# W_out's block sums laid out by product, made over the first chunk of the second layer, and read into twelve buffers

## The chip, the cores and the metric

The kernel runs on one core of a Trainium2 chip. The metric is device time in microseconds (us) of one execution. The engines are TensorE (PE; its weight loads PEld run beside it), VectorE (DVE), ScalarE (ACT), GpSimd (POOL) and SyncE (SP, which here only issues DMAs); transfers run on 16 DMA engines.

## What is computed

Windowed attention over 4 batches x 8 heads x 576 positions x 64 elements, then two feed-forward layers on the 2304 x 512 result. All of it is float32.

```python
x = attention(q, k, v)                 # causal, window of 64; reshaped to [2304, 512]
h = x @ w_in                           # [512, 2048]
x = (h * sigmoid(h)) @ w_out           # [2048, 512]
h = x @ w_in2                          # second layer
g = where(h >= 1, h, where(h <= -1, 0, (h + 1)**2 / 4))
out = g @ w_out2                       # [2304, 512]
```

## The kernel before

**Products.** Every float32 operand is split into a high part of type fp32r and the rest (`hi_lo`, L758 for the rest; the high part is a copy, L261 on ACT or L263 on DVE), and a product is three matmuls: high by low, low by high, high by high. The weights of both layers come as pairs of 32-bit words and are converted once (`weight`, L315 to L385); the second layer's go to DRAM (`ws2`).

**Layer 1** takes the tokens in five chunks (512, 256, 512, 512, 512), with the attention between them. `step` (L676) multiplies by W_in (L688), applies the activation on ACT twice, once to float32 and once to fp32r (L698, L700), subtracts on DVE (L702) and multiplies by W_out (L722).

**Layer 2** takes the tokens in three chunks n of 768, in two halves of 384 (TH). W_in's product is a block product in seven products (tokens: `tokens_quarters`, weights: `weights_quarters`, with sums L762). In chunk n=0 the 2048 hidden units are taken in eight pairs (`pair`, L856): seven products of six matmuls (L872), sums on DVE (L880), the activation (L899 DVE, L901 ACT, L903 DVE, cast on ACT, L905 DVE), then a plain product with W_out (L944) whose weights are W_out's high and low parts. The block sums of W_in are stored in `a_dram` (L832) and read again (L816) for n=1 and n=2, whose first product is made phase by phase (L1020, sums L1028) before the second.

**W_out for n=1 and n=2.** Their second product is a block product in seven products too: `products_out` (L1089) runs 7 x 8 = 56 units of six matmuls (L1143), and each unit reads its own piece of W_out's block sums, high and low, of 256 KB. `weights_out(i)` makes them for pair i: it loads the two pieces of W_out (`wst`, L970), splits them (these parts also serve n=0's L944), forms four sums in place, splits those, and stores all of it in `e_dram` (L976). A unit's load (L1104) takes 256 of a row's 512 columns, high and low, so a partition's 2 KB lie in DRAM as two runs of 1 KB. The loads go round a ring of 7 buffers (`TAGS`), those of the first product's weights.

**The order** is set by a list scheduler (class `Plan`). Each operation has a key, made of its step's due time and a term of the table K; a cost on each engine that could run it; `lat`, what the planner adds for a DMA to land; and `after`, before which it isn't put. The planner puts at each moment the ready operation with the lowest key on each engine and writes one fixed order for each engine. So a waiting instruction holds all that stands behind it on its engine. The time in the plan decides the order alone; on the chip, semaphores do. `lead2` (102.98) lets W_out's loads for pair i start that many planned us before pair i's due time, and so in layer 1.

**Output.** Each finished tile is turned by DVE (L1111) and stored by four DMAs of 48 KB (L1116), on SP except for the very last.

Of the kernel before, what the change touches and what calls it, by code (L numbers as in the profile page):

```python
# [10 lines left out]
F32 = mybir.dt.float32  # L11
# [34 lines left out]
class Plan:  # L46
# [128 lines left out]
K = dict(wload=-19.78, rebias=0.22, low=-18.2, shift=-27.36, add=-0.16, sign=10.81, hi=-2.67, lo=-23.79, qkv=-15.09,  # L175
         v=1.07, qT=-26.02, kT=0.97, sc=-21.48, max=-20.9, exp=-6.11, sum=-40.26, tr=-13.39, pv=1.78, x=-11.84,
         f_max=-1.34, f_exp=29.66, f_sum=2.76, f_tr=21.88, f_pv=3.83, f_x=6.87, f_v=7.59, f_t0=-4.04, f_t1=6.08,
         f_t2=44.33, f_t3=13.71, f_a0=-25.21, f_a1=16.54, f_a2=20.65, f_a3=22.2, f_l0=-24.76, f_l1=-19.36, f_l2=4.46,
         f_l3=20.84, f_v0=-20.48, f_v1=-20.39, f_v2=0.67, f_v3=1.42, split=-8.01, x2=-61.84, act=13.29, sub=-6.21,
         out=3.75, w2=-6.13, t0=29.25, drift0=0.58, drift1=0.86, pu0=0.33, pu1=0.61, pu2=0.34, pu3=0.52, c1=30.89,  # L180
         stay=36.55, spare=4.5, evac=26.68, base2=-5.58, store=9.98, bhl=-13.0, bsub=7.66, aload=22.2, fload=-50.69,
         ahl=44.73, asum=24.32, astore=-7.2, add2=-12.87, act2=-4.15, sub2=8.31, out2=32.34, wi0=163.69,
         ahead2=-59.06, lead2=102.98, w22=-35.28, ehl=-5.54, esum=6.04, estore=-37.75, hadd=-26.88, hact=1.31,
         s1=8.57, ring=-3.45, osum=-51.98, oload=-55.71, oev=12.85, ostore=3.95, bq=56.81)
# [19 lines left out]
def tile_window_attention_two_ffn(  # L204
# [110 lines left out]
    def weight(layer, f, part, key, early, after=0.0):  # L315
# [49 lines left out]
        op(key + K["wload"], dict(sp=1.45 if part else 1.71), load, w=[hi, lo], makes=[st], lat=1.9, after=after)  # L365
# [404 lines left out]
    def tokens_quarters(n):  # L770

        at = lambda nm: T2[0] + PAIR * order[nm] / 7 if not n else H0[n] + UNIT * order1[nm] + K["bq"]
        key = H0[n]
        for a in range(2):
            x = {}
            for h in range(2):
                for kk in (a, a + 2):
                    nm = f"b{kk // 2 + 1}{h + 1}"
                    b = x[nm] = Buf(xp, "xf", [128, 512])
                    t0 = n * WIDE + h * TH  # L780
                    need = [item for p0, p1, item in x2_parts[kk] if p0 < t0 + TH and p1 > t0]
# [18 lines left out]
            keep("t2", x["b22"])  # L800
            keep("b21", x["b21"])
            minus("t4", x["b21"], x["b21"], x["b22"])
            keep("t4", x["b21"])

    def weights_quarters(n, i):
# [7 lines left out]
        if n:  # L813
            for nm, _ in IN_BANKS:
                y = aq[n, i, nm]
                op(at(nm) + K["aload"], dict(sp=0.35), lambda e, nm=nm: e.dma_start(out=whole(nm), in_=a_dram[i, nm][:, :]),  # L816
                   r=[("a", i, nm)], w=[(y, 0), (y, 1)], makes=[y], lat=2)
            return
        w = []
        for f in (2 * i, 2 * i + 1):  # L820
            b = Buf(wp, "wf", [128, 512])
            w.append(b)
            op(key + K["fload"], dict(sp=0.75), lambda e, b=b, f=f: e.dma_start(out=b.t, in_=ws2[0][f][:, :]),
               r=[("ws2", 0, f)], w=[(b, 0), (b, 1)], makes=[b], lat=2)
# [137 lines left out]
    e_dram = {(i, x): dram.tile([128, 2, 512], F32, name=f"e_{i}_{x}") for i in range(NF // 2) for x in range(4)}  # L962

    def weights_out(i):
# [10 lines left out]
        def store(x, y, halves):  # L975
            op(t + K["estore"], dict(sp=0.35), lambda e: e.dma_start(out=e_dram[i, x][:, :, 0:256 * halves],  # L976
                                                                    in_=y.t[:, :, 0:256 * halves].bitcast(F32)),
               r=[(y, 0), (y, 1)], w=[("e", i, x)], lat=2)

        store(0, wt[1, 2 * i, 1], 1)  # L980
        store(1, wt[1, 2 * i + 1, 1], 2)

# [8 lines left out]
        for x in range(2):  # L991
            y = Buf(wp, "w0", [128, 2, 512], F32R)
            hi_lo(t + K["ehl"], lambda part, y=y: y.t[:, part, :], lambda x=x: w.t[:, x, :], 512, [(w, x, 0), (w, x, 1)], (y,), [y])
            store(2 + x, y, 2)
# [91 lines left out]
    IN_OUT = dict(P1=(0, 0, 0), P5=(1, 2, 0), P6=(0, 3, 1), P7=(1, 2, 1), P2=(2, 1, 0), P3=(0, 1, 1), P4=(3, 3, 0))  # L1086
    TAGS = ((ap, "qn"), (ap, "kn"), (ap, "qT"), (ap, "kT"), (ap, "pT"), (ap, "pT"), (ap, "v"))

    def products_out(n):  # L1089
# [9 lines left out]
        for j, (q, x, half) in enumerate(products):  # L1099
            for i in range(NF // 2):  # L1100
                s = (NF // 2) * j + i
                pool, tag = TAGS[s % 7] if not (last and j == 6 and i == 7) else (xp, "xf")
                y = ew[j, i] = Buf(pool, tag, [128, 2, 256], F32R)
                op(at_o(n, j, i) + K["oload"], dict(sp=0.35), lambda e, y=y, i=i, x=x, half=half: e.dma_start(  # L1104
                    out=y.t.bitcast(F32), in_=e_dram[i, x][:, :, half * 256:half * 256 + 256]),
                   r=[("e", i, x)], w=[(y, 0), (y, 1)], makes=[y], lat=2)

        def store(j, m, src, r, c):
# [185 lines left out]
```

## Time and profile before

| | |
|---|---|
| median of 3 runs | 903.74 us (903.32 to 905.78) |
| the profiled execution, its own time | 902.7 us |
| its span, first to last instruction | 900.9 us |
| mean granted TensorE clock | 0.987 |
| busy: PE, DVE, ACT, POOL | 95%, 71%, 58%, 12% of the span |

The page of the profile gives busy times of the engines and the costliest groups of instructions. The trace behind it can be asked for windows (busy time of each engine in a stretch, the granted clock, the DMA engines' busy share), timelines (instructions of an engine in order, with the idle time ahead of each and what ended it), waits (that idle time summed by what ended it) and DMAs. By the timeline, layer 1 ends at about 511 us, chunk n=0 takes 493 to 636, n=1 to 772 and n=2 the rest; the layers overlap at 486 to 513.

### The profile page before, as it was taken

The numbers are of one execution on the slowest core, as the hardware profiler recorded it, in microseconds if no ns is written. First come the engines' busy times: TensorE is split into PE (matmuls) and PEld (weight loads), VectorE is DVE, ScalarE is ACT, GpSimd is POOL, SyncE is SP. The second block draws the span as 40 slices with busy tenths as digits, with TensorE's granted clock in tenths as the row PEclk, the third lists the DMA queues.
The fourth block names the chain that finished last, engine by engine and source line by source line (L and its number), as shares of the span: only waits on it lengthen the run. The fifth ranks groups of instructions, "written<-read, shape, count | busy, mean of one in ns | idle before, by whom it ended". The sixth has DMA issues, their size and how long they took to land.

```text
span 900.9 us, 16116 instructions
## 1 busy us (share of the span) xinstructions
PE 858.6 (95%) x5470; PEld 758.0 (84%) x5470; DVE 638.1 (71%) x1519; ACT 526.7 (58%) x1148; POOL 107.4 (12%) x111
## 2 busy tenths in 40 slices
PE   7899999999999999999998899999999998899996
PEld 6788778998778887888886798888899998899996
DVE  5899996655564367535677699778877984678951
ACT  6989987866675378733435444444566631567430
POOL 3100100100000000000000233113022010113010
PEclk9999999999999999999999899999999999999998
DMA  9952535654566056503678766438788789887786
GB/s 259 326 172 70 156 71 121 154 132 105 148 168 151 24 163 191 139 14 100 210 274 312 272 251 229 164 129 297 242 246 254 238 267 237 246 252 246 234 235 139
DMA packets 231602, 172.00 MB, mean 191 GB/s; under 512 B 141152, under 2 KB 191840, under 8 KB 231520
## 3 DMA queue, kind: packets, MB, share of 16 engines
q1 hardware_dynamic: 230320, 170.83, 63.7%
q8 instruction: 43, 0.70, 0.3%
q14 instruction: 39, 0.32, 0.1%
q10 hardware_dynamic: 1200, 0.15, 0.1%
HBM read 123.73 MB, written 47.19 MB: 190 GB/s over the span
## 4 chain that ended last, share of the span: by engine, by line
PE 54%; DMA 14%; ACT 13%; DVE 10%; SPq 6%; issue 3%; POOL 0%; DVEq 0%; ACTq 0%; POOLq 0%
PE acc L722 11%; PE h L688 11%; PE acc L1020 6%; PE acc L1143 6%; PE h L872 5%; PE at L1020 3%; PE acc L944 3%; DMA wst<-ws 2%; DMA w<-in_moe_w_in_dram 2%; ACT s L421 2%; PE at L1143 2%; PE h L1143 2%; DVE w L758 2%; ACT L421 2%; ACT wl L338 1%
## 5 line engine op out<-in xcount | busy, mean ns | idle before, releaser
L722 PE MATMUL acc<-g,w 128*128 128x512 f32 (+1 forms) x996 | 222.5, 367 | 0.0
L688 PE MATMUL h<-xt,w 128*128 128x512 f32 (+1 forms) x996 | 215.6, 364 | 1.8 <-ACT g L700 1.8
L688 PEld LDWEIGHTS h<-xt,w 128*128 128x128 f32 x996 | 169.6, 189 | 32.4 <-ACT g L700 3.0
L722 PEld LDWEIGHTS acc<-g,w 128*128 128x128 f32 x996 | 169.1, 190 | 29.5 <-issue 2.1
L702 DVE TENSOR_TENSOR g<-gf,g 128x512 fp32r<-128x512 f32 (+1 forms) x83 | 52.6, 634 | 44.6 <-ACT g L700 44.2
L698 ACT ACTIVATE gf<-h 128x512 f32<-128x512 f32 (+1 forms) x83 | 44.8, 540 | 55.7 <-PE h L688 55.3
L261 ACT CAST w<-w 128x384 fp32r<-128x384 f32 x75 | 36.8, 511 | 26.9 <-PE acc L1143 18.3
L421 ACT ACTIVATE s<-s,st 128x128 f32<-128x128 f32 x128 | 49.9, 392 | 4.2 <-DVE st L400 3.9
L417 POOL TENSOR_TENSOR s<-s,st 128x512 f32<-128x512 f32 (+1 forms) x16 | 15.8, 986 | 287.7 <-DVE st L414 163.0
L346 DVE CUSTOM_DVE_ANT_0 wf<-wf,wl 128x1024 uint16<-128x1024 uint16 x64 | 45.0, 704 | 2.3 <-ACT wl L338 1.4
L700 ACT ACTIVATE g<-h 128x512 fp32r<-128x512 f32 (+1 forms) x83 | 44.7, 538 | 2.8 <-PE acc L722 2.7
L1020 PE MATMUL acc<-w,pT 128*128 128x384 f32 x192 | 39.3, 340 | 2.5 <-DMA pT<-a_s 1.9
L758 DVE TENSOR_TENSOR w<-w,w 128x384 fp32r<-128x384 f32 x67 | 34.6, 548 | 7.7 <-ACT w L261 7.7
L338 ACT ACTIVATE wl<-wst 128x512 int32<-128x512 uint32 x32 | 21.5, 671 | 29.7 <-DMA wst<-in_moe_w_out_dram 12.8
L698 ACT ACT_TABLE_LOAD x27 | 34.6, 1283 | 5.1 <-PE h L688 4.6
L1020 PEld LDWEIGHTS acc<-w,pT 128*128 128x128 f32 x192 | 33.9, 188 | 3.8 <-DVE xt L1120 1.3
L421 ACT ACT_TABLE_LOAD x28 | 35.9, 1283 | 0.5
L880 DVE TENSOR_TENSOR xt<-h,xt 128x384 f32<-128x384 f32 x56 | 30.6, 552 | 6.5 <-PE h L872 5.7
L1028 DVE TENSOR_TENSOR w<-acc,xt 128x384 f32<-128x384 f32 x48 | 26.7, 556 | 11.2 <-PE acc L1020 10.0
L400 DVE CUSTOM_DVE_ANT_0 s<-at,mask 128x128 f32<-128x128 f32 x128 | 29.2, 282 | 6.2 <-PE at L531 6.2
L342 DVE TENSOR_SCALAR wf<-wf 128x512 int32<-128x512 int32 x48 | 20.2, 429 | 18.6 <-ACT wf L333 18.2
L944 PE MATMUL acc<-w,g 128*128 128x512 f32 x120 | 31.9, 393 | 0.1
(238 smaller groups left out, 1716.8 us busy)
## 6 DMA issues: line engine op xcount, KB each, us to landing
e<-w SPq DMA_DIRECT2D x24, 512.0 KB, 4.2
w<-in_moe_w_in_dram SPq DMA_DIRECT2D x16, 512.0 KB, 7.3
w<-in_moe_w_out_dram SPq DMA_DIRECT2D x16, 512.0 KB, 7.1
wst<-in_moe_w_in_dram SPq DMA_DIRECT2D x16, 512.0 KB, 4.3
ws<-wf SPq DMA_DIRECT2D x32, 256.0 KB, 4.4
wst<-in_moe_w_out_dram SPq DMA_DIRECT2D x16, 512.0 KB, 4.1
pT<-a_s SPq DMA_DIRECT2D x32, 256.0 KB, 3.1
pT<-e SPq DMA_DIRECT2D x32, 256.0 KB, 3.5
```

The lines of the kernel that those rows point to most:

```text
L346: e.tensor_tensor(out=i, in0=i, in1=wl.t, op=ALU.add)
L421: e.activation(out=s.t[:, jj, :], in_=s.t[:, jj, :], func=AF.Exp, scale=-1.0, bias=st.t[:, jj:jj + 1], accum_out=st.t[:, 4 + jj:5 + jj])
L688: e.matmul(out=h.t[:, 0:n], lhsT=w[:, a, kk, :], rhs=xt[layer, c, kk // 2].t[:, kk % 2, b, lo:hi], start=(kk == 0 and j == 0), stop=(kk == ...
L698: op(key, dict(act=t_act(n, True)), lambda e: e.activation(out=gf.t[:, 0:n], in_=h.t[:, 0:n], func=AF.Silu), r=[h], w=[gf], makes=[gf], ta ...
L700: op(key, dict(act=t_act(n, True)), lambda e: e.activation(out=g.t[:, 0, 0:n], in_=h.t[:, 0:n], func=AF.Silu), r=[h], w=[(g, 0)], makes=[g ...
L702: op(T[i] + K["sub"], dict(dve2=t_dve(n)), lambda e: e.tensor_tensor(out=g.t[:, 1, 0:n], in0=gf.t[:, 0:n], in1=g.t[:, 0, 0:n].bitcast(F32) ...
L722: e.matmul(out=acc[t].t[:, lo:hi], lhsT=wo.t[:, a, t * 128:(t + 1) * 128], rhs=g.t[:, b, 0:n], start=fresh and j == 0, stop=(j == 2 and f ...
L758: op(key, dict(dve2=t_dve(n), pool=0.18 + 2.17e-3 * n), lambda e: e.tensor_tensor(out=y(1), in0=src(), in1=y(0).bitcast(F32), op=ALU.subtr ...
L872: e.matmul(out=acc(nm), lhsT=y.t[:, p, a * 128:a * 128 + 128], rhs=bq[n, bn, a].t[:, q, :], start=(a == 0 and j == 0), stop=(a == 1 and j ...
L944: e.matmul(out=acc2[quarter % 2 * 3 + m].t, lhsT=y(p)[:, m * 128:m * 128 + 128], rhs=wo.t[:, q, :], start=(f == 0 and j == 0), stop=(f == ...
L1020: e.matmul(out=acc(nm), lhsT=y.t[:, p, a * 128:a * 128 + 128], rhs=bq[n, bn, a].t[:, q, :], start=(new and a == 0 and j == 0), stop=(a == ...
L1143: e.matmul(out=banks[j][m].t[:, 0:TH], lhsT=w.t[:, p, m * 128:m * 128 + 128], rhs=y.t[:, r, :], start=(j < 4 and i == 0 and k == 0), stop= ...
```

## The change

In words:

- `e_dram` is cut by product: each unit's piece, high and low, is one run of 2 KB for each partition. The three plain blocks B11, B21, B22 have tiles of their own, the sums lie with the half outermost (and are split into that order). Stores go from 32 to 40 of the same bytes in all.
- W_out's loads for pair i start `lead3` = 21.25 planned us before its due time instead of 102.98, so the block sums are made pair by pair over chunk n=0.
- The ring has 12 buffers: two of `wf`, one of `wl` and two of `gf` are added, which are free by then.
- The planner's costs: a DMA issue on SP 0.4 where 0.75 stood, `lat` 3 to 4 where 2 stood. Tokens of n=1 and n=2 are split no earlier than 22 us ahead of their chunk.
- K's numbers are others; among them `wi0` 163.69 to 211.15 (the second layer's weights are converted later in layer 1).
- Every output store may go on ACT's queue or SP's.

```diff
 # weight, second layer
-        op(key + K["wload"], dict(sp=1.45 if part else 1.71), load, ..., lat=1.9, after=after)
+        op(key + K["wload"], dict(sp=0.45 if layer else 1.45 if part else 1.71), load, ..., lat=3.8 if layer else 1.9, after=after)
 # tokens_quarters
-                hi_lo(at(nm) + K["bhl"], ..., TH, [src], (y,), [y])
+                hi_lo(at(nm) + K["bhl"], ..., TH, [src], (y,), [y],
+                      H0[n] - 22 if n else 0.0)
 # weights_quarters
-            op(key + K["fload"], dict(sp=0.75), ..., lat=2)
+            op(key + K["fload"], dict(sp=0.4), ..., lat=3.4)
 # weights_out
-    e_dram = {(i, x): dram.tile([128, 2, 512], F32, ...) for i in range(NF // 2) for x in range(4)}
+    e_dram = {(i, x): dram.tile([128, 2, 2, 256], F32, ...) for i in range(NF // 2) for x in range(2)}
+    e_dram.update({(i, x): dram.tile([128, 2, 256], F32, ...) for i in range(NF // 2) for x in ("B11", "B21", "B22")})
-               ..., makes=[] if x else [w], lat=2, after=T2[i + 1] - K["lead2"])
+               ..., makes=[] if x else [w], lat=4, after=T2[i + 1] - K["lead3"])
-        store(0, wt[1, 2 * i, 1], 1)
-        store(1, wt[1, 2 * i + 1, 1], 2)
+        for name, x, half in (("B11", 0, 0), ("B21", 1, 0), ("B22", 1, 1)):
+            y = wt[1, 2 * i + x, 1]
+            store(name, y, lambda y=y, half=half: y.t[:, :, 256 * half:256 * half + 256])
-            y = Buf(wp, "w0", [128, 2, 512], F32R)
+            y = Buf(wp, "w0", [128, 2, 2, 256], F32R)
-            store(2 + x, y, 2)
+            store(x, y, lambda y=y: y.t)
 # products_out
-    TAGS = ((ap, "qn"), (ap, "kn"), (ap, "qT"), (ap, "kT"), (ap, "pT"), (ap, "pT"), (ap, "v"))
+    TAGS = ((ap, "qn"), (ap, "kn"), (ap, "qT"), (ap, "kT"), (ap, "pT"), (ap, "pT"), (ap, "v"), (wp, "wf"), (wp, "wf"),
+            (wp, "wl"), (gp, "gf"), (gp, "gf"))
-                    out=y.t.bitcast(F32), in_=e_dram[i, x][:, :, half * 256:half * 256 + 256]),
-                   ..., lat=2)
+                    out=y.t.bitcast(F32), in_=e_dram[i, x] if half is None else e_dram[i, x][:, half, :, :]),
+                   ..., lat=3.2)
-                op(t + K["ostore"], dict(sp=0.35, act=0.35) if last and j == 6 and m else dict(sp=0.35), ...
+                op(t + K["ostore"], dict(sp=0.55, act=0.55), ...
```

Lines after L757 move on by a few: L758 becomes L759, L762 L763, L880 L882, L905 L907, L1104 L1110, L1116 L1122.

How the order of the instructions moves, at three places. First ACT at the seam of the layers, where the last activations of layer 1 (`gf<-h`, `g<-h`) stand; `w<-wst` is a split of W_out, `w<-xf` of tokens, `qn<-wf` and the like of W_in's sums. Before:

```order
L261 CAST w_5786<-xf 128x384
L261 CAST w_5795<-xf 128x384
L261 CAST w_5800<-wst 128x512
L261 CAST w_5804<-wst 128x512
L698 ACTIVATE gf<-h 128x512
L700 ACTIVATE g<-h 128x512
L261 CAST w_5854<-wst 128x512
L698 ACTIVATE gf<-h 128x512
L700 ACTIVATE g<-h 128x512
L261 COPY xt<-h 128x384
L261 CAST qn<-wf 128x256
```

And with the change:

```order
L261 CAST kn<-wl 128x256
L261 CAST pT<-wf 128x256 x2
L261 CAST w_5705<-xf 128x384
L698 ACTIVATE gf<-h 128x512
L700 ACTIVATE g<-h 128x512
L698 ACTIVATE gf<-h 128x512
L700 ACTIVATE g<-h 128x512
L698 ACTIVATE gf<-h 128x512
L700 ACTIVATE g<-h 128x512
L261 COPY xt<-h 128x384
L261 CAST kn<-wl 128x256
```

The splits of W_out between the last activations are gone; they stand behind them, one pair at a time.

Second, POOL in chunk n=0, about one pair of it. Before, seven instructions:

```order
L758 TENSOR_TENSOR v<-wf,v 128x256
L758 TENSOR_TENSOR qT<-wf,qT 128x256
L762 TENSOR_TENSOR wl<-wf 128x256
L762 TENSOR_TENSOR wl<-wl,wf 128x256
L762 TENSOR_TENSOR wf<-wf,wl 128x256
L758 TENSOR_TENSOR pT<-wf,pT 128x256
L758 TENSOR_TENSOR qn<-wf,qn 128x256
```

And with the change, seven of which two (on `wst`) are of W_out:

```order
L759 TENSOR_TENSOR w_6388<-wst,w_6388 128x512
L763 TENSOR_TENSOR wst<-wst 128x256
L763 TENSOR_TENSOR wl<-wf 128x256
L763 TENSOR_TENSOR wl<-wl,wf 128x256
L763 TENSOR_TENSOR wf<-wf 128x256
L759 TENSOR_TENSOR kn<-wl,kn 128x256
L759 TENSOR_TENSOR pT<-wf,pT 128x256
```

In the whole chunk, from the first sum of the first product (L880, now L882) to the first of n=1 (L1028, now L1032), POOL has 52 instructions where it had 39 and DVE 257 where it had 244; from the third pair on, a pair has 31 on DVE and these 7 on POOL.

Third, SP in the last chunk's second product: `e_...` are the loads of W_out's pieces, `out_dram` the stores. Before:

```order
L1104 DMA qn<-e_3_182 128x2x256
L1116 DMA out_dram<-s 32x12x32 x2
L1104 DMA kn<-e_3_186 128x2x256
L1116 DMA out_dram<-s 32x12x32 x2
L1104 DMA pT<-e_3_198 128x2x256
L1116 DMA out_dram<-s 32x12x32 x2
L1104 DMA qT<-e_3_190 128x2x256
L1116 DMA out_dram<-s 32x12x32 x2
L1104 DMA v<-e_1_172 128x2x256
L1104 DMA kT<-e_3_194 128x2x256
```

And with the change:

```order
L1110 DMA wl<-e_1_182 128x512
L1122 DMA out_dram<-s 32x12x32 x2
L1110 DMA gf<-e_1_184 128x512
L1122 DMA out_dram<-s 32x12x32
L1110 DMA pT<-e_B_200 128x512
L1110 DMA gf<-e_1_186 128x512
L1110 DMA pT<-e_B_203 128x512
L1110 DMA qn<-e_B_188 128x512
```

Three stores stand between the loads where eight stood. Of the 64 stores of `products_out`, ACT's queue has 36 and SP's 28; before, SP's had 61. On ACT they stand in groups of 5, 5, 5, 4 in chunk n=1 and 5 and 12 in n=2, between the casts of the activation.

## Rows read from the trace of the kernel before

**Rows 1.** The page's busy times (us, share of the span) and instructions.

```profile
PE 858.6 (95%) x5470; PEld 758.0 (84%) x5470; DVE 638.1 (71%) x1519; ACT 526.7 (58%) x1148; POOL 107.4 (12%) x111
```

**Rows 2.** Timeline of PE at the seam: start, us, instruction, [idle before <-what ended it].

```profile
492.93 2.29 PE L872 MATMUL h<-w,qn 128*128 128x384 f32 x6 [3.53 <-ACT g L700]
...
502.84 1.31 PE L872 MATMUL h<-w,kT 128*128 128x384 f32 x6 [1.27 <-DVE xt L880]
...
507.90 3.70 PE L872 MATMUL h<-w,pT 128*128 128x384 f32 x12 [3.06 <-DVE xt L880]
```

**Rows 3.** Timeline of ACT at the seam.

```profile
490.22 0.62 ACT L261 CAST w<-wst 128x512 fp32r<-128x512 f32 x1 [2.47 <-DMA wst<-ws]
...
501.45 0.40 ACT L261 CAST qn<-wf 128x256 fp32r<-128x256 f32 x1 [5.72 <-DMA wf<-ws]
```

**Rows 4.** Windows: us, busy PE PEld DVE ACT POOL, PE clock, DMA share, GB/s.

```profile
490.00:495.00 5.00, 2.07 (x6) 2.07 (x7) 4.26 (x10) 3.72 (x7) 0.00 (x0) 0.65 1.01 371
495.00:500.00 5.00, 5.00 (x18) 4.41 (x18) 3.78 (x9) 0.48 (x1) 0.00 (x0) 0.67 1.02 375
...
510.00:515.00 5.00, 5.00 (x23) 4.57 (x22) 3.57 (x9) 2.85 (x6) 2.50 (x3) 0.80 0.48 181
755.00:760.00 5.00, 5.00 (x23) 5.00 (x22) 1.48 (x3) 0.51 (x1) 0.00 (x0) 0.73 0.94 229
880.00:885.00 5.00, 4.70 (x18) 4.70 (x19) 0.00 (x0) 0.00 (x0) 0.00 (x0) 0.66 0.54 141
```

**Rows 5.** Waits of PE, 640 to 772 us: us in total, times, longest.

```profile
PE acc L1143 <- DMA qn<-e: 2.0, 1, 2.0
PE acc L1143 <- DMA v<-e: 1.5, 1, 1.5
PE acc L1020 <- DMA pT<-a_s: 1.0, 1, 1.0
PE at L1143 <- DMA v<-e: 0.6, 1, 0.6
PE acc L1143 <- DMA kn<-e: 0.5, 1, 0.5
```

**Rows 6.** Waits of PE, 772 to 901 us.

```profile
PE at L1143 <- DMA v<-e: 3.8, 1, 3.8
PE acc L1020 <- DMA pT<-a_s: 0.9, 1, 0.9
```

**Rows 7.** Timeline of SP: a load of W_in, two stores, a load of W_out.

```profile
691.24 0.32 SPq L816 DMA_DIRECT2D v<-a_a  x1
...
868.62 1.10 SPq L1116 DMA_DIRECT2D out_dram<-s  x2
...
875.34 0.52 SPq L1104 DMA_DIRECT2D v<-e  x1
```

**Rows 8.** DMAs issued in 700 to 764 and in 772 to 828: KB each, median us to landing.

```profile
pT<-e SPq DMA_DIRECT2D x14, 256.0 KB, 3.7
...
pT<-a_s SPq DMA_DIRECT2D x14, 256.0 KB, 3.0
```

**Rows 9.** Windows: the first chunk; a stretch mostly of the second product; one mostly of the first.

```profile
510.00:636.00 126.00, 125.37 (x606) 109.82 (x604) 107.20 (x226) 60.24 (x136) 33.91 (x36) 0.99 0.56 202
...
700.00:764.00 64.00, 59.18 (x319) 56.74 (x318) 49.73 (x94) 25.99 (x55) 5.41 (x6) 0.97 0.85 246
764.00:828.00 64.00, 61.50 (x346) 60.32 (x345) 46.11 (x92) 37.91 (x83) 12.63 (x9) 1.00 0.82 248
```

**Rows 10.** Timeline of SP at the end.

```profile
889.55 8.63 SPq L1116 DMA_DIRECT2D out_dram<-s  x13
```

**Rows 11.** Timelines of POOL and DVE in the first chunk, the same instructions in time.

```profile
521.05 2.98 POOL L758 TENSOR_TENSOR w<-wst,w 128x512 fp32r<-128x512 f32 x2
...
515.46 0.55 DVE L905 TENSOR_TENSOR g<-gf,g 128x384 fp32r<-128x384 f32 x1
...
521.47 1.40 DVE L905 TENSOR_TENSOR g<-gf,g 128x384 fp32r<-128x384 f32 x1 [0.16 <-ACT g L261]
```

More of the change, by code (lines that the diff above doesn't have):

```diff
@@ L169, in emit @@
             o.fn(engines[e])
[L175 to L184, printed above, removed]
+K = dict(lead3=21.25, wload=-19.75, rebias=0.22, low=-18.2, shift=-27.36, add=-0.16, sign=10.81, hi=-2.67, lo=-23.79,
+         qkv=-15.09, v=1.07, qT=-26.02, kT=0.97, sc=-21.48, max=-20.9, exp=-6.11, sum=-40.26, tr=-13.39, pv=1.78,
+         x=-11.84, f_max=-1.34, f_exp=29.66, f_sum=2.76, f_tr=21.88, f_pv=3.83, f_x=6.87, f_v=7.59, f_t0=-4.04,
+         f_t1=6.08, f_t2=44.33, f_t3=13.71, f_a0=-25.21, f_a1=16.54, f_a2=20.65, f_a3=22.2, f_l0=-24.76, f_l1=-19.36,
+         f_l2=4.46, f_l3=20.84, f_v0=-20.48, f_v1=-20.39, f_v2=0.67, f_v3=1.42, split=-8.01, x2=-42.55, act=13.29,
+         sub=-6.21, out=3.75, w2=-6.13, t0=29.25, drift0=0.58, drift1=0.86, pu0=0.33, pu1=0.61, pu2=0.34, pu3=0.52,
+         c1=30.89, stay=36.55, spare=4.5, evac=31.71, base2=-6.76, store=44.34, bhl=-18.08, bsub=-1.93, aload=19.77,
+         fload=-94.29, ahl=55.17, asum=2.36, astore=-29.92, add2=-17.14, act2=-9.14, sub2=10.02, out2=-0.03,
+         wi0=211.15, ahead2=-64.36, lead2=102.98, w22=-48.69, ehl=15.82, esum=5.93, estore=-76.04, hadd=-122.23,
+         hact=0.93, s1=8.06, ring=-15.86, osum=-117.16, oload=-65.77, oev=43.71, ostore=7.82, bq=55.04)
 def t_act(n, psum=False):
@@ L364, in weight @@
         hi, lo = (st, 1), (st, 0)
-        op(key + K["wload"], dict(sp=1.45 if part else 1.71), load, w=[hi, lo], makes=[st], lat=1.9, after=after)
+        op(key + K["wload"], dict(sp=0.45 if layer else 1.45 if part else 1.71), load, w=[hi, lo], makes=[st], lat=3.8 if layer else 1.9, after=after)
         op(key + K["rebias"], dict(act=t_act(512) + 0.045, dve2=0.6), rebias, r=[hi], w=[w], makes=[w])
@@ L376, in weight @@
         if layer:
-            op(key + K["store"], dict(sp=0.75), lambda e: e.dma_start(out=ws2[part][f][:, :], in_=w.t), r=[w],
-               w=[("ws2", part, f)], lat=2)
+            op(key + K["store"], dict(sp=0.45), lambda e: e.dma_start(out=ws2[part][f][:, :], in_=w.t), r=[w],
+               w=[("ws2", part, f)], lat=3.8)
             return
@@ L822, in weights_quarters @@
             w.append(b)
[L823 to L824 removed]
+            op(key + K["fload"], dict(sp=0.4), lambda e, b=b, f=f: e.dma_start(out=b.t, in_=ws2[0][f][:, :]),
+               r=[("ws2", 0, f)], w=[(b, 0), (b, 1)], makes=[b], lat=3.4)
         ss = Buf(wp, "wl", [128, 512])
@@ L1115, in store @@
                 to = bass.AP(out.tensor, out.offset + t0 * C + c0 + 32 * b, [[C, 32], [32 * C, 12], [1, 32]])
-                op(t + K["ostore"], dict(sp=0.35, act=0.35) if last and j == 6 and m else dict(sp=0.35), lambda e, b=b, to=to: e.dma_start(out=to, in_=y.t[b * 32:b * 32 + 32, :, :]),
+                op(t + K["ostore"], dict(sp=0.55, act=0.55), lambda e, b=b, to=to: e.dma_start(out=to, in_=y.t[b * 32:b * 32 + 32, :, :]),
                    r=[y], lat=2)
```

39 lines of the change are left out of this document (21 added, 18 removed).

## The prediction, made before the changed kernel was run

> **What bounds the kernel now.** I read the page's busy times first: PE works 858.6 of 900.9 us [rows 1], so the kernel is a queue of matmuls, and only what idles PE or lowers its clock can change the time. About 42 us of the span are left. The next view is PE's own timeline and waits in the second layer, the part that the change touches, and then the windows with the granted clock, because PE at a lower clock counts as busy.
>
> At the **seam of the layers** PE stops three times: 3.53 us for an activation of layer 1 on ACT, and 1.27 and 3.06 us for sums of the first product on DVE [rows 2], 7.86 together. ACT's timeline tells why: the activation that PE wants stands behind a split of W_out (`w<-wst`), which waits 2.47 us for its load; a cast of W_in's quarters waits 5.72 us for its own load [rows 3]. Both loads come late since the DMA engines are full there, share 1.01 and 1.02, moving 371 to 375 GB/s [rows 4]: W_out's pieces, their block sums and the first chunk's data in one place. After these stops the clock drops. A busy stretch at a granted clock of c gives away (1 - c) of its length: 2.07 x 0.35 + 5.00 x 0.33 + 5.00 x 0.20 = 3.4 us in the three windows of the seam [rows 4]; 0.65 to 0.80 there is a mean over the lower and the upper level (1.2 and 2.4 GHz). The seam loses 11.2 us.
>
> In **the second products** of n=1 and n=2 PE waits for loads of W_out's pieces: 2.0, 1.5, 0.6 and 0.5 us in n=1 [rows 5], 3.8 us in n=2 [rows 6]; and at the start of each first product for a load of W_in's sums, 1.0 and 0.9 us [rows 5, 6]. The two long ones again cost clock: 5.00 x 0.27 = 1.35 and 4.70 x 0.34 = 1.6 us [rows 4].
>
> Why the pieces are late can be counted. 346 matmuls took 61.50 us [rows 9], 0.178 each, so a unit of six takes 1.07 us. With 7 buffers a buffer comes back after 7.5 us, of which one unit reads it; 6.4 us remain for a new load, and it needs 0.52 us of issue [rows 7] and 3.7 us to land [rows 8]. SP may thus fall behind by 2.2 us. Eight output stores at 1.10 us for two [rows 7] are 4.4 us.
>
> **The change, part by part.** *Seam.* W_out's splits leave the place between the last activations, as the order of ACT shows, and the block sums' traffic goes to n=0, where the DMA share is 0.56 [rows 9]. Of the 3.53 us I take 3.0 (DVE's subtraction and a table load stay near); of the 4.33 for the sums of the first product 3.9, as the casts wait for loads on emptier engines; of the 3.4 of clock 3.0, since the clock fell after the stops. Gain 9.9; the bounds are 0 (another load comes late in their stead) and 11.2.
>
> *Twelve buffers and whole pieces.* With 12 buffers a load has 12 x 1.07 - 1.07 = 11.8 us, so SP may fall behind by about 7.5, more than the 4.4 of eight stores. A contiguous load of the same 256 KB, W_in's, takes 0.32 to issue where W_out's takes 0.52 [rows 7], and lands in 3.0 us, not 3.7 [rows 8]; I expect W_out's loads to become like that. Of the waits I take 4.1 of 4.6 in n=1 and 3.6 of 3.8 in n=2. The first loads of W_in's sums need buffers that the ring gives back, and the ring now holds them for a smaller share of its units: 0.5 of each, 1.0 together, bounds 0 and 1.9. With the waits the lower clock goes: 1.3 and 1.5. Together 4.1 + 3.6 + 1.0 + 2.8 = 11.5. Bounds: 0, and all of it, 13.3.
>
> The Trainium skill, "DMA: Bandwidth & Descriptors", section "Specifications", puts the smallest transfer for line rate at 512 B; by it runs of 1 KB are as good as 2 KB, and the layout would bring nothing. The trace agrees as far as the share goes, and the rows on landing don't; by either the sum above is the same as long as the buffers do the work, and they part in the first rival.
>
> *Stores on two queues.* SP has 28 of them and not 61, so between the last loads three where eight stood. At the end SP issues 13 stores in 8.63 us, at 0.66 each [rows 10], and the change's order still has 12 there; I take 0.5 for the end, bounds 0 and 2. The move costs ACT 36 x 0.55 = 20 us of issue, and ACT is busy 25.99 of 64 us in the second product and 37.91 in the first [rows 9], so its idle time covers that, unless a store waits (third rival).
>
> *W_out in n=0.* Now PE loses 0.6 of 126 us there. DVE is busy 107.20 us with 226 instructions, 0.474 each, and POOL 33.91 with 36, 0.94 each [rows 9]. The order gives each engine 13 more in the chunk: 6.2 us for DVE and 12.2 for POOL, so DVE goes to about 113 of 126 and ACT, at 60.24, has room. Cover is there, but it is thin: where a sum of the first product is late on DVE, PE waits. I take 3 us, bounds 0 and 8 (the 6.2 of DVE on the path with some of POOL's beside it); beyond that is the second rival.
>
> *Layer 1 and the rest.* The weights of layer 2 are converted later and the order on every engine is another. Layer 1 shows no wait on which I could put a gain; I take a loss of 0.5, bounds -4 and 2. For new waits at the turns of the chunks and for stores that hold ACT I take 1.5, bounds 0 and 5.
>
> **Sum.** -9.9 - 11.5 - 0.5 + 3 + 0.5 + 1.5 = -16.9. Against the profiled execution's 902.7 us that is 885.8; the median of the runs is 1.0 above it, so 886.8, **887 us**. With every gain at its upper bound and no cost it would be 902.7 - 11.2 - 13.3 - 2 + 1.0 = 877.2, less up to 4 in layer 1: 873 to 874.
>
> **The rivals.** *First: the DMA engines pace the second product, and buffers don't help.* For it: their share is 0.85 at 246 GB/s over the stretch [rows 9] and 0.94 where PE came out of its wait [rows 4]. Against it: the same engines moved 375 GB/s at the seam [rows 4], half as much again. Then the waits stay and with them the clock, 4.1 + 3.6 + 2.8 = 10.5 us less gain, of which the shorter landing gives back up to 0.7 for each of the five waits (0.6 and 0.5 for the small ones), 3.2: 887 + 7.3 = 894. By the rule of 512 B quoted from the Trainium skill nothing comes back, and it would be 897.
>
> *Second, slower: DVE and POOL hold each other up in n=0.* Two subtractions on POOL took 2.98 us, and the DVE instruction beside them 1.40 where the same one takes 0.55 [rows 11]. A pair lasts 126 / 8 = 15.75 us. From the third pair on it has 31 DVE instructions, 31 x 0.474 = 14.7 us, and 7 on POOL, 6.6 us. If DVE can't run while POOL does, that is 21.3 us, 5.55 too much, and over five such pairs 28 us: 887 - 3 + 28 = 912, slower than before. It begins to cost as soon as more than 15.75 - 14.7 = 1.05 us of POOL's 6.6 block DVE, and it decides the sign when some 5 us do. Against it: POOL already worked 33.91 us beside DVE's 107.20, 141 us in 126, and PE lost 0.6 [rows 9], so the two do overlap, and DVE's mean of 0.474 already holds what it suffered.
>
> The Trainium skill has this as a rule: "SBUF — State Buffer", section "Who interferes with whom", says that the two engines share a pair of ports under an exclusive lock, and that a DVE instruction with two operands from SBUF is kept out by a GpSimd instruction that reads SBUF, one with a single operand from there not. The rows of the one stretched instruction agree; many of DVE's here take one operand from PSUM, and by the rule those go on.
>
> *Third: stores hold ACT.* A store on ACT waits for DVE's turn of its tile, and behind it stand casts that PE wants. If half of the 36 x 0.55 = 20 us falls on such casts, 10 us are lost: 897. For it: groups of five stand in front of casts in n=1. Against it: ACT is idle over half of that stretch [rows 9].
>
> *Fourth: the stops only move.* The seam keeps its traffic from the first pair, another load is late, and the chunk n=0 pays what the second products save: 901 to 906, no change to speak of.
>
> **How the numbers follow.** My forecast has a chance of 0.62, with a range of its own of 876 to 893; the first rival 0.10, the second 0.09, the third 0.12, the fourth 0.07. A measurement of this kernel can tell 0.3%, 2.7 us, from no change. Forecast, first and third are faster: 0.84. Same is the fourth, 0.07; slower is the second, 0.09. The range is 874 to 901: it takes in the bounds of the costs and the first and third rivals, and leaves out the second, the fourth and 0.04 below or above, 0.2 in all.
>
> **What would show it.** Right: at the seam no wait of PE over 1 us and a clock above 0.9 in its windows; in the second products waits for loads of W_out under 1 us together in each chunk and no window below 0.9; the loads issued in about 0.32 us and landed in about 3.0; in n=0 PE idle for 2 to 5 us in waits for sums on DVE, DVE at about 113 us. Wrong: over 8 us of waits for DVE in n=0, with POOL above 45 us and DVE's mean above 0.5 us (second rival); waits for loads as long as before with the DMA share above 0.9 (first); PE waiting for ACT's casts ahead of the groups of stores (third); a stop over 3 us at the seam for a load of the first pair (fourth).

## The result, and the profile after

The changed kernel takes 877.0 us (median of 4 runs, 874.3 to 878.3); the kernel before, in the same comparison, 904.75. The ratio is 0.969 (95% interval 0.966 to 0.972): faster by 3.1%. It lies inside the range (874 to 901) and 10 us below the forecast of 887. The profiled execution took 878.1 us, its span 876.3 us where it was 900.9.

The page's busy times, to set beside [rows 1]:

```profile
PE 845.9 (97%) x5470; PEld 752.7 (86%) x5470; DVE 642.2 (73%) x1519; ACT 521.4 (59%) x1137; POOL 125.6 (14%) x125
```

The same 5470 matmuls, 12.7 us less busy time (some 7 of it the clock, whose mean rises from 0.987 to 0.995; the rest is not traced) and 11.9 us less idle time. To see where, I counted matmuls in windows of 3 us in both traces and asked when PE had begun the k-th. The table gives that difference to the kernel before at points on the kernel before's clock, in us; it is good to about 1 us, since the order of the matmuls differs a little.

| at | 485 | 515 | 602 | 662 | 722 | 764 | 797 | 863 | end of span |
|---|---|---|---|---|---|---|---|---|---|
| after | -1.0 | -12.8 | -12.7 | -14.8 | -16.2 | -20.5 | -16.9 | -18.0 | -24.6 |

The seam (485 to 515) gives 11.8, chunk n=0 costs nothing, the second product of n=1 gives about 5, the turn to n=2 takes 3.6 back, the second product of n=2 gives the rest.

**The seam.** PE's timeline there, to set beside [rows 2]; no group has an idle time ahead of it, and every group runs at its full pace:

```profile
485.28 2.89 PE L688 MATMUL h<-xt,w 128*128 128x512 f32 x12
488.00 1.23 PE L874 MATMUL h<-w,qn 128*128 128x384 f32 x6
489.07 0.86 PE L722 MATMUL acc<-g,w 128*128 128x512 f32 x3
489.76 1.23 PE L874 MATMUL h<-w,kn 128*128 128x384 f32 x6
```

**The windows** (us, busy PE PEld DVE ACT POOL, clock, DMA share, GB/s), to set beside [rows 4, 9]:

```profile
480.00:510.00 30.00, 30.00 (x147) 26.57 (x147) 24.35 (x50) 13.31 (x29) 7.22 (x8) 1.00 0.76 272
510.00:636.00 126.00, 125.06 (x623) 112.31 (x622) 119.31 (x237) 69.38 (x154) 46.12 (x45) 1.00 0.83 291
...
700.00:764.00 64.00, 56.77 (x316) 55.05 (x314) 45.31 (x96) 19.83 (x42) 10.90 (x9) 1.00 0.88 259
764.00:828.00 64.00, 63.66 (x352) 63.35 (x353) 52.55 (x100) 39.82 (x87) 13.60 (x9) 0.97 0.78 238
```

The block sums' traffic has moved: n=0 now has a DMA share of 0.83 where it had 0.56. DVE works 119.3 of 126 us there and PE still 125.06. But 700 to 764 has become worse, 56.77 us of PE where [rows 9] have 59.18. The window now takes in the turn from n=1 to n=2: the first product of n=2 begins at 739.77 us where it began at 762.64.

**The waits of PE** from 640 to 772 us, to set beside [rows 5]:

```profile
PE at L1024 <- DMA qn<-a_a: 2.1, 1, 2.1
PE acc L1024 <- DMA pT<-a_s: 2.0, 1, 2.0
PE at L1024 <- DMA qT<-a_a: 1.6, 1, 1.6
PE acc L1024 <- DMA kT<-a_s: 1.1, 1, 1.1
PE h L1024 <- DMA kn<-a_s: 0.5, 1, 0.5
```

All waits for W_out's pieces (L1143 before, L1149 now) are gone, here and in 772 to 876, where no wait is left at all. In their place stand 7.3 us of waits for W_in's sums (L1024) at the turn from n=1 to n=2, where there were 1.9 (1.0 in [rows 5] and 0.9 in [rows 6]), and a lower clock after them. This new wait is what the experiments turn on.

SP's timeline and its waits at the turn show what held the loads:

```profile
752.11 0.38 SPq L1122 DMA_DIRECT2D out_dram<-s  x1
752.75 0.34 SPq L818 DMA_DIRECT2D kn<-a_s  x1
756.16 0.85 SPq L1122 DMA_DIRECT2D out_dram<-s  x2
757.10 1.27 SPq L818 DMA_DIRECT2D qT<-a_a  x1
```

```profile
SPq L818 <- PE acc L1024: 7.1, 8, 1.5
SPq L1122 <- DMA out_dram<-s: 4.8, 3, 3.1
SPq L1110 <- DMA out_dram<-s: 2.7, 2, 1.5
```

SP stands still from 753.1 to 756.2 in front of a store. It waits not for that store's data but for the completion of another store, one that ACT had issued: in the program, DMAs take their completion semaphores in turn, and each waits until the one that used its semaphore before, eight DMAs ago, has landed, on whichever queue that was. The trace bears this out: it has eight such semaphores, ACT's store of 752.10 us landed at 756.14, and SP issued the store that takes the same semaphore at 756.16. The load of `qT` stands behind it, and PE waits 1.64 us for it. The first of the waits, 2.1 us for `qn`, began in the same way: SP's store of 736.24 us follows the landing, at 736.22, of a store that ACT had issued at 730.74, and the load of `qn` stands behind it.

### The profile page after: what moved, and what is told of

It is laid out like the page before. It is cut to its first block, busy times and chain, and to the rows that moved or that the text cites. A ratio compares the mean times of both kernels' runs of the same rounds, so it can differ in the third digit from the quotient of the medians.

```text
span 876.3 us, 16140 instructions
## 1 busy us (share of the span) xinstructions
PE 845.9 (97%) x5470; PEld 752.7 (86%) x5470; DVE 642.2 (73%) x1519; ACT 521.4 (59%) x1137; POOL 125.6 (14%) x125
## 4 chain that ended last, share of the span: by engine, by line
PE 65%; DMA 11%; DVE 9%; ACT 9%; SPq 4%; issue 2%; POOL 0%; DVEq 0%; ACTq 0%; POOLq 0%
PE h L688 14%; PE acc L722 13%; PE acc L1024 8%; PE acc L1149 7%; PE h L874 5%; PE at L1149 4%; PE at L1024 4%; PE acc L946 3%; PE h L1149 2%; DMA ws<-wf 2%; PE h L1024 2%; PE at L946 2%; DMA qn<-in_q_dram 2%; ACT L421 1%; SPq L483 1%
## 5 line engine op out<-in xcount | busy, mean ns | idle before, releaser
L702 DVE TENSOR_TENSOR g<-gf,g 128x512 fp32r<-128x512 f32 (+1 forms) x83 | 52.1, 628 | 46.1 <-ACT g L700 45.5
L261 ACT CAST w<-w 128x384 fp32r<-128x384 f32 x73 | 34.9, 510 | 25.1 <-PE acc L1149 12.0
L1024 PE MATMUL acc<-w,pT 128*128 128x384 f32 x192 | 39.2, 339 | 2.8 <-DMA pT<-a_s 2.0
L759 DVE TENSOR_TENSOR w<-w,w 128x384 fp32r<-128x384 f32 x68 | 34.7, 547 | 6.1 <-ACT w L261 6.1
L1024 PEld LDWEIGHTS acc<-w,pT 128*128 128x128 f32 x192 | 34.0, 188 | 3.4 <-DMA pT<-a_s 2.4
L1032 DVE TENSOR_TENSOR w<-acc,xt 128x384 f32<-128x384 f32 x48 | 26.5, 555 | 13.3 <-PE acc L1024 12.3
L882 DVE TENSOR_TENSOR xt<-h,xt 128x384 f32<-128x384 f32 x56 | 30.1, 547 | 1.7 <-PE h L874 1.6
L1063 DVE TENSOR_TENSOR w<-w,xt 128x384 f32<-128x384 f32 x48 | 28.7, 608 | 2.3 <-ACT xt L1055 1.2
```

What stands on the lines that cost most here:

```text
L261: nc.scalar.copy(out=out, in_=in_)
L702: op(T[i] + K["sub"], dict(dve2=t_dve(n)), lambda e: e.tensor_tensor(out=g.t[:, 1, 0:n], in0=gf.t[:, 0:n], in1=g.t[:, 0, 0:n].bitcast(F32) ...
L1024: e.matmul(out=acc(nm), lhsT=y.t[:, p, a * 128:a * 128 + 128], rhs=bq[n, bn, a].t[:, q, :], start=(new and a == 0 and j == 0), stop=(a == ...
```

## The experiments

"Ratio" is to the kernel before in the same comparison; that kernel's own median was between 904.8 and 909.6 us in them, so ratios are compared, not times. Each planner change lets the scheduler write a new order, so waits are read from each trace.

**1. The ring of 7 again.**

```diff
-TAGS = (..., (ap, "v"), (wp, "wf"), (wp, "wf"), (wp, "wl"), (gp, "gf"), (gp, "gf"))
+TAGS = (..., (ap, "v"))
```

> The changed kernel with the ring of 7 buffers again, all else as changed. Theory (the buffers removed the waits for W_out's pieces in the second products): of the 8.4 us of such waits of before most come back, 5 to 9 us with the clock that falls after them, 882 to 887 us; the seam stays without a wait. Rival (the whole 2 KB runs and the stores taken off SP removed them): 875 to 879, no wait over 1 us for W_out's pieces.

Ratio 0.967 (0.964 to 0.970), as the changed kernel's. The waits of PE from 640 to 780 and from 780 on:

```profile
PE acc L1148 <- DMA kn<-e: 2.6, 2, 2.2
PE acc L1024 <- DVE w L1063: 1.6, 1, 1.6
...
PE at L1148 <- DMA v<-e_B: 1.7, 1, 1.7
```

With 0.4 and 0.3 more, 5.0 us of waits for W_out's pieces come back, as the theory said, but the 7.3 us of waits for loads at the turn are gone (2.0 us for DVE and ACT stand there). So with the stores as the change has them, the ring of 12 moves a wait from one load to the other and gains nothing. The theory had the first half only.

**2. W_out's loads early again.**

```diff
-  after=T2[i + 1] - K["lead3"]
+  after=T2[i + 1] - K["lead2"]
```

> The changed kernel with W_out's loads allowed 102.98 planned us ahead again, so in layer 1. Theory (the block sums' place made the stops at the seam): waits of 5 to 8 us at the seam and the lower clock return, 886 to 890 us. Rival (the later conversion of the second layer's weights, that is the table K and the longer latencies of the planner, removed them): 875 to 879 and no wait over 1 us at the seam.

Ratio 0.984 (0.979 to 0.988): this part is worth some 13 us (9 to 17 by the interval), half of the whole gain. PE's waits in 480 to 516 and in 516 to 640:

```profile
PE h L874 <- ACT xt L261: 3.1, 1, 3.1
PE h L874 <- DVE xt L882: 1.9, 1, 1.9
...
PE h L874 <- DVE kT L759: 4.0, 1, 4.0
PE acc L946 <- DVE g L907: 2.2, 3, 1.2
```

The stops at the seam return, and with the new table they run on into chunk n=0, whose first 50 us have PE busy for 43.78 at a clock of 0.94 and a DMA share of 0.90:

```profile
510.00:560.00 50.00, 43.78 (x195) 37.23 (x195) 42.92 (x93) 21.92 (x48) 13.17 (x11) 0.94 0.90 320
```

By the matmul count this kernel is 9.9 us ahead of the one before at 515 and 0.9 behind it at 545.

**3. The stores on SP alone.**

```diff
-  dict(sp=0.55, act=0.55)
+  dict(sp=0.55, act=0.55) if last and j == 6 and m else dict(sp=0.55)
```

> The changed kernel with the output stores on SP alone (but for the last, as before). Theory (the new waits of 7.3 us for loads of W_in's sums at the turn to n=2 come from stores on two queues: SP's own store waits for the completion of one on ACT and holds the loads behind it): these waits fall below 3 us; 12 buffers take up the longer queue on SP, so waits for W_out's pieces stay under 1 us; 870 to 876 us. Rival A (the ring of 12 gives the loads of W_in's sums their buffers too late): the turn keeps 5 to 8 us, 876 to 880. Rival B (SP's queue was what made W_out's pieces late): 2 to 5 us of waits for them in n=2 return, 879 to 883.

Ratio 0.961 (0.958 to 0.963), 871.75 us, span 869.7: faster than the change. Waits at the turn fall from 7.3 to 3.2 (`kT<-a_s` 1.9, `pT<-a_s` 1.3); SP no longer waits for the completion of a store there. No wait for W_out's pieces came. The theory stands as far as two queues cost more than they save; a rest of 3.2 is left, in between theory and rival A.

**4. The old layout of e_dram, with 12 buffers** (the tiles, the stores, `IN_OUT` and the loads as before the change; the longer latency kept).

> The changed kernel with e_dram laid out as before, loads in runs of 1 KB, ring of 12. Theory (the layout is worth little once there are 12 buffers): loads issue in 0.52 us and land 0.5 us later than with whole pieces, and no wait over 1 us comes of it: 876 to 880 us. Rival (the layout carried it): waits of 3 to 8 us for W_out's pieces, 881 to 888.

Ratio 0.967 (0.964 to 0.970), as the changed kernel. The loads issue in 0.52 us where whole pieces take 0.32 and land in 3.5 us (median, `pT<-e`, 640 to 720) where those take 3.2. Waits for W_out's pieces: 0.7 us together; the turn keeps 6.5 (the profiled execution, 884.4 us, was the slowest of five; the median is 879.6). With 12 buffers the layout changes the loads and not the time; with 7 it was not tried by itself.

**5. The table alone: all four parts undone.**

> The changed kernel with its four parts undone: ring of 7, runs of 1 KB, W_out's loads 102.98 planned us ahead, stores on SP; what is left is the planner's table, costs and latencies. Theory (the parts carry the gain): stops of 5 to 8 us at the seam and 6 to 9 us of waits for W_out's pieces, ratio to the kernel before 0.985 to 1.0. Rival (the planner's longer latencies and the table carry half of it or more): ratio 0.97 to 0.983.

Ratio 0.984 (0.977 to 0.992), between the two; the interval holds both. So the planner's table, costs and latencies bring part of the gain by themselves, and how much can't be told from this interval. It is the ratio of experiment 2, where only W_out's loads were put back: undoing the ring, the layout and the two queues as well costs nothing that the intervals show. In the trace the span is 891.9, 9.0 us shorter: 5.8 us of stops at the seam, 3.8 us of waits in n=0, and 6.8 us of waits for W_out's pieces, against 9.3 before (small ones included).

**6. No POOL in the first chunk's weights.**

```diff
+    side = lambda n: {} if no_pool[0] else dict(pool=0.18 + 2.17e-3 * n)
-        op(key, dict(dve2=t_dve(n), pool=0.18 + 2.17e-3 * n), ...
+        op(key, dict(dve2=t_dve(n), **side(n)), ...
```

`no_pool[0]` is set while the first chunk's parts of W_in and W_out are planned.

> The changed kernel in which the weights' splits and sums of the first chunk never go to POOL (W_in's and W_out's; the planner puts all on DVE). It weighs the second rival: DVE works 119.3 of 126 us there beside 46.1 us of POOL in 45 instructions. If the two overlap freely, these 45 cost DVE some 0.45 us each, 20 us, so DVE needs 139 us: PE waits 10 to 15 us more, ratio 0.98 to 0.987. If POOL's time is taken from DVE through a shared port, DVE gets back what it gives: 0 to 4 us, ratio 0.966 to 0.974.

Ratio 0.977 (0.970 to 0.984), between the two. The window of n=0:

```profile
510.00:636.00 126.00, 119.76 (x574) 105.56 (x573) 115.39 (x268) 57.73 (x131) 11.69 (x10) 0.97 0.77 269
```

From 525 to 585 us PE is full in both kernels, so DVE's work can be compared there: 147 instructions in 58.7 us without POOL, 123 in 59.9 us with POOL, which did 29 beside them. So POOL took next to no time off DVE: most of what was handed over, DVE lost beside it. As an estimate: at what each shape takes on DVE without POOL (415, 550 and 682 ns for two operands of 256, 384 and 512 elements, 351 for one of 384), those that began on DVE in these 60 us lost 10.0 us beside POOL, and the 27 that began on POOL would have cost DVE 12.5. The groups of DVE's instructions in 516 to 606 us, by shape (busy, mean ns of one), first with POOL, then without, show which lost:

```profile
L882 DVE TENSOR_TENSOR xt<-h,xt 128x384 f32<-128x384 f32 x40 | 21.3, 545 | 0.4 <-PE h L874 0.3
L759 DVE TENSOR_TENSOR w<-wst,w 128x512 fp32r<-128x512 f32 x15 | 14.7, 978 | 0.0
...
L759 DVE TENSOR_TENSOR v<-wf,v 128x256 fp32r<-128x256 f32 x5 | 6.5, 1296 | 0.0
L907 DVE TENSOR_TENSOR xt<-gf,xt 128x384 fp32r<-128x384 f32 x5 | 4.9, 981 | 0.0
L759 DVE TENSOR_TENSOR pT<-wf,pT 128x256 fp32r<-128x256 f32 x6 | 2.5, 412 | 0.0
```

```profile
L885 DVE TENSOR_TENSOR xt<-h,xt 128x384 f32<-128x384 f32 x36 | 19.4, 551 | 1.6 <-PE h L877 1.2
L762 DVE TENSOR_TENSOR w<-wst,w 128x512 fp32r<-128x512 f32 x19 | 12.5, 683 | 0.0
...
L762 DVE TENSOR_TENSOR pT<-wf,pT 128x256 fp32r<-128x256 f32 x11 | 4.3, 415 | 0.0
L910 DVE TENSOR_TENSOR xt<-gf,xt 128x384 fp32r<-128x384 f32 x5 | 2.7, 549 | 0.0
...
L762 DVE TENSOR_TENSOR v<-wf,v 128x256 fp32r<-128x256 f32 x6 | 2.5, 416 | 0.0
```

`v<-wf,v`, both operands from SBUF, took 1296 ns beside POOL and 416 without; `xt<-h,xt`, with `h` from PSUM, 545 and 551. Single instructions of the changed kernel, in 510 to 636 us, show it more sharply: the 27 `xt<-h,xt` that had POOL at work beside them for over a quarter of their time took 546 ns, as the other 21 did, and the four `v<-wf,v` beside it 1515 where two alone took 418. Not every instruction with two operands from SBUF lost: five `pT<-wf,pT` beside POOL took 411 (their group 412 with POOL, 415 without). The Trainium skill, "SBUF — State Buffer", section "Who interferes with whom", says that a DVE instruction with two inputs from SBUF contends with a GpSimd instruction that reads SBUF, and that one with at most one such input doesn't, outside DVE's 2-port modes. The trace agrees for `v<-wf,v` and `xt<-h,xt`.

What this kernel lost it lost late: PE waits 5.9 us for DVE's `g` in the last pairs (one of 4.6), and the clock falls after it, to 0.77 in 615 to 630. That wait isn't a full DVE alone: DVE itself stood still for 2.99 us ahead of it, for ACT, and ACT for a load of tokens:

```profile
617.48 0.56 DVE L762 TENSOR_TENSOR w<-xf,w 128x384 fp32r<-128x384 f32 x1 [2.99 <-ACT w L261]
...
616.94 0.92 ACT L261 CAST w<-xf 128x384 fp32r<-128x384 f32 x2 [3.57 <-DMA xf<-x]
```

Until 585 us PE was as busy without POOL as with it.

**7. The ring of 7 and the stores on SP alone** (edits 1 and 3 together).

> The changed kernel with the ring of 7 and the stores on SP alone. With 7 buffers and stores on both queues the second products waited 5.0 us for W_out's pieces and the turn 0; with 12 and SP alone 0 and 3.2. Theory (a ring of 7 leaves SP 2.2 us to fall behind, and eight stores take more): waits for W_out's pieces of 5 to 9 us and the clock after them, none for W_in's sums: ratio 0.967 to 0.975. Rival (the waits came from stores on two queues with common completion semaphores, the ring is of no use): no wait over 1 us of either kind, ratio 0.956 to 0.960.

Ratio 0.965 (0.959 to 0.971): waits for W_out's pieces 4.7 us, at the turn 0.2. The waits are about those of the theory (5 to 9 us); the ratio lies between theory and rival, and the gap to the ring of 12 with these stores (0.961) isn't clear of the intervals.

**8. Five buffers for the last product of n=1.**

```diff
-  pool, tag = TAGS[s % len(TAGS)] if not (last and ...
+  pool, tag = (TAGS[7 + i % 5] if j == 6 and not last else TAGS[s % len(TAGS)]) if not (last and ...
```

with the stores on SP alone.

> Ring of 12, stores on SP, and in the last product of n=1 only the five added buffers, so that the seven of W_in's sums come free eight units earlier for n=2. Theory (at the turn the loads of W_in's sums wait for buffers that the ring of 12 still holds): the 3.2 us of waits there with stores on SP go, 0 to 1 us are left, ratio 0.955 to 0.959. Rival (stores between the loads on SP hold them): the waits stay at 2 to 4 us, or W_out's pieces are late for five buffers: ratio 0.960 to 0.966.

Ratio 0.963 (0.958 to 0.969); one load of W_in's sums (`kn<-a_s`) is waited for 3.8 us, and 0.7 for another. The buffers came free earlier and the waits stayed, as the rival had it.

**9. The stores on ACT alone** (but for the last product).

```diff
-  dict(sp=0.55, act=0.55)
+  dict(sp=0.55, act=0.55) if last and j == 6 else dict(act=0.55)
```

> The changed kernel with the output stores on ACT alone (but for the last product, where either may take them); SP then only loads. Theory (the DMAs of both queues take the eight completion semaphores in turn, so a load on SP waits for a store on ACT that itself waits): SP still waits for stores' completions, 2 to 7 us of PE waits for W_in's sums at the turn remain, ratio 0.963 to 0.972. Rival (SP's own stores in front of the loads hold them): the turn has no wait over 1 us, ratio 0.953 to 0.960 unless ACT's casts come late.

Ratio 0.965 (0.961 to 0.969). SP, which issues no store there, still waits 4.5 us in two places for a store's completion (`SPq L818 <- DMA out_dram<-s`): the common turn of the completion semaphores is shown. PE's waits at the turn are 1.2 us for a load and 2.3 for a copy that ACT makes late: as much as is lost with the stores on SP alone, in another place. The theory's 2 to 7 us for the loads was too much.

**10. A store planned at 1.2 us on SP.**

```diff
-  ... else dict(sp=0.55)
+  ... else dict(sp=1.2)
```

on top of edit 3; the planner then puts one store to two loads where it put one to one.

> Ring of 12, stores on SP alone, and the planner told 1.2 us for a store on SP instead of 0.55, so that it puts one store to two loads where it put one to one. Theory (SP issues without a pause at the turn, and loads stand behind stores): the 3.2 us of waits for W_in's sums that stores on SP left fall below 1.5, ratio 0.955 to 0.960. Rival (the ring of 12 gives the buffers too late, or the DMA engines are full there, share 0.95): the waits stay at 2 to 5 us, ratio 0.960 to 0.966.

869.4 us, span 865.7, ratio 0.962 (0.959 to 0.965). The windows from 640 us:

```profile
640.00:700.00 60.00, 60.00 (x343) 60.00 (x342) 52.23 (x99) 40.82 (x92) 12.70 (x8) 1.00 0.80 250
700.00:764.00 64.00, 64.00 (x365) 63.92 (x364) 48.91 (x100) 26.08 (x54) 14.42 (x12) 1.00 0.92 272
764.00:828.00 64.00, 63.86 (x362) 63.11 (x361) 58.13 (x113) 39.24 (x85) 7.83 (x6) 1.00 0.86 265
```

PE has no wait in 640 to 780 and none after; with a DMA share of 0.92 in the second product. So neither the buffers nor the DMA engines' throughput made the loads late: SP's order of stores and loads did. The ratio is not the theory's (0.955 to 0.960): it is that of experiment 3, though the profiled span is 4.0 us shorter, so what the last 3.2 us of waits are worth in time is not shown.

**11. The kernel before with the ring of 12 alone.**

> The kernel before with nothing changed but the ring, 12 buffers for 7. Theory (the ring moves waits from W_out's pieces to W_in's sums): the 8.4 us of waits for W_out's pieces fall below 2, 2 to 6 us come up at the turn, the seam stays: ratio 0.990 to 1.0. Rival (by itself it is worth its 10 us): no new wait at the turn, ratio 0.983 to 0.989.

Ratio 0.993 (0.989 to 0.996). Waits for W_out's pieces fall to 0.4 us; at the turn one load of W_in's sums (`qn<-a_a`) is waited for 5.9 us and the next chunk has 1.5; the seam keeps 7.8. What held that load is in SP's timeline, eight stores in a row in front of it, and then PE's:

```profile
750.08 6.54 SPq L1117 DMA_DIRECT2D out_dram<-s  x8
...
757.95 0.59 SPq L816 DMA_DIRECT2D qn<-a_a  x1
...
763.00 2.26 PE L1020 MATMUL at<-w,qn 128*128 128x384 f32 x6 [5.85 <-DMA qn<-a_a]
```

The theory holds: a wait is moved, and a few us are left over.

**12. Experiment 10 with the ring of 7.**

> The kernel with stores on SP alone at a planned 1.2 us, which had no wait of PE over 0.6 us in the whole second layer, with the ring of 7 for 12. Theory (7 buffers leave SP 2.2 us to fall behind, 12 leave 7.5): waits for W_out's pieces of 3 to 6 us and some clock come back, ratio 0.965 to 0.972, 3 to 8 us slower than with 12. Rival (with the stores spread out, the ring's size is of no account): no wait over 1 us, ratio 0.958 to 0.964.

868.1 us, ratio 0.959 (0.957 to 0.961). Waits for W_out's pieces 1.2 us together, none over 0.8. The theory falls: with the stores spread out, 7 buffers do as well as 12. This kernel, experiment 10's and experiment 3's beat the changed one; between the three there is no difference that the intervals show.

## Why the prediction was right, and where it was wrong

Against the profiled execution I forecast -16.9 us and it was -24.6 (902.7 to 878.1). The medians add 2.1: before's was 1.0 above its profiled execution, after's 1.1 below. By the steps:

- **The seam, -9.9: right, and a little more.** PE's stops and the lower clock are gone entirely, -11.8 by the matmul count; the upper bound of 11.2 left out a clock of 0.85 on 2.10 us of PE in 505 to 510, and the rest is within the count's error. That W_out's place did it is shown by experiment 2, where putting it back brings stops at the seam and costs half of the whole gain. That the table could carry part of it I had not counted (experiment 5: its stops at the seam are 5.8 us for 7.9).
- **Chunk n=0, +3: wrong, it was about 0.** Of the stretches of the span this is the largest miss; from 485 to 662 us the count gives -13.8 where seam and chunk were forecast at -6.9. The step that failed is "where a sum of the first product is late on DVE, PE waits", with DVE at "about 113 of 126". DVE went to 119.3, in some windows of 15 us it worked 14.97, and PE was busy for 15.00 of them:

```profile
525.00:540.00 15.00, 15.00 (x76) 13.42 (x76) 14.96 (x31) 7.91 (x19) 6.88 (x7) 1.00 0.72 259
...
570.00:585.00 15.00, 15.00 (x76) 13.46 (x76) 14.97 (x31) 8.50 (x21) 6.97 (x7) 1.00 0.92 315
```

 A full engine isn't a late one: the added work is not on PE's path of the moment (W_out's parts for later pairs and chunks), and the sums that PE wants stand ahead of it in DVE's order (read from the order, not tried by itself).
- **The second rival** (912 us) rested on the block between DVE and POOL, and that block is real, larger in the single instruction than the 1.40 of 0.55 in [rows 11]: 1296 ns for 416. Two of its signs came, POOL above 45 us (46.1) and DVE's mean above 0.5 (119.3 us for 237 instructions), the third, 8 us of waits for DVE, did not (0.2). What failed was 31 x 0.474 + 6.6 with no overlap: in a window of 15 us, 31 instructions took DVE 14.97 us beside 6.97 of POOL. `xt<-h,xt` isn't held by POOL at all, and of the instructions with two operands in SBUF only some are.
- **Buffers and whole pieces, -11.5: the waits nearly right, the reasons not.** The waits for W_out's pieces did go, all 8.4 of them with their clock, where I took 7.7. But the count of slack, 2.2 us with 7 buffers against 7.5 with 12, made the ring their cause, and it isn't needed: with the stores spread out a ring of 7 does the same (experiment 12), and with dense stores a ring of 12 only moves the wait to W_in's sums (experiments 1 and 11). My own figure said so: a burst of stores against 2.2 us of slack. I credited the slack and not the burst. Whole pieces brought no time with 12 buffers (experiment 4), though they issue in 0.32 as I had expected. That they land 0.7 us sooner I had read from two different stretches; in one stretch, 640 to 720 us, `pT<-e` lands in 3.4 before and 3.2 after. Of the two readings that I set against each other in the first rival the Trainium skill's, "DMA: Bandwidth & Descriptors", section "Specifications", 512 B, fits the time better.
- **W_in's sums at the turn, -1.0: the wrong sign.** 7.3 us of waits stand where 1.9 stood. Those 1.9 I had read as one wait at the start of each first product; both belong to n=2, as PE's timeline before shows:

```profile
770.70 1.30 PE L1020 MATMUL acc<-w,pT 128*128 128x384 f32 x6 [0.98 <-DMA pT<-a_s]
...
781.87 1.30 PE L1020 MATMUL acc<-w,pT 128*128 128x384 f32 x6 [0.94 <-DMA pT<-a_s]
```

 And now there is a clock of 0.66 to pay for:

```profile
765.00:770.00 5.00, 5.00 (x21) 5.00 (x21) 2.40 (x5) 2.93 (x6) 1.01 (x1) 0.66 0.39 129
```

 I had put 1.5 us on new waits and the stores together. That the stretch from 662 us to the end comes out at -9.8, where the terms for it add up to -10.5, is in part luck: the turn cost some 7 us (7.3 - 1.9, and 1.7 of clock) where I had put 0.5, and gains that no term lists make up for it.
- **Stores on two queues, -0.5: a loss.** I wrote that ACT's idle time covers them unless a store holds ACT. The place was wrong: the stores held SP, whose DMAs wait for theirs. On SP alone they are worth 0.961 against 0.969, some 7 us. The end of the span is 0.7 us shorter, as forecast.
- **Layer 1, +0.5:** -1.0, within its bounds.

The first rival (the DMA engines pace the second product) is refuted by experiment 10: PE full at a share of 0.92. The third was half right: held queues cost some 7 us where it said 10, on another engine, and were outweighed. The fourth, that the stops only move, is what experiment 2 shows for the new table with W_out early; it is not what the change did.

Still open: how much of the gain the table alone carries (experiment 5's interval is 14 us wide); and the new table without W_out's move can't be taken apart further, since the planner's terms work on each other.

## What to carry to other kernels

Before adding buffers for a load that comes late, look at what stands in front of it on its queue: here spreading the stores between the loads left 1.2 us of waits with 7 buffers, and 12 buffers without that only moved the wait. Work may be put beside a full PE until the helping engine is busy nearly all the time, as here (119.3 of 126 us), if it stands behind what PE wants in that engine's order; that the order is the reason was not tried by itself. Moving DMAs to a second queue frees issue time, but where all DMAs take common completion semaphores in turn, a load on one queue then waits for a store on the other.

## What the runs showed of the hardware

- DVE with POOL at work and without, means of groups over 90 us: 1296 ns for 416, 981 for 549, 978 for 683, but also 412 for 415, in instructions with both operands in SBUF; 545 for 551 with one in PSUM. Over the same 60 us, 24 instructions fewer on DVE and 29 on POOL left DVE as busy as without POOL, 59.9 us for 58.7.
- Two runs of 1 KB or one of 2 KB for each partition made a load of 256 KB issue in 0.52 or 0.32 us and land in 3.5 or 3.2, with no effect on the kernel's time (with 12 buffers).
- PE stayed fully busy through 64 us with a DMA share of 0.92 at 272 GB/s.
